# Windowed attention and channel mixing: low parts of weights and the first unit's mixing on TensorE and ScalarE

## The chip, the cores and the metric

The kernel runs on one core of one Trainium2 chip. The metric is device time in microseconds (us) of one execution. The engines have short names here, as in the profile: PE is TensorE (PEld its weight loads), DVE is VectorE, ACT is ScalarE, POOL is GpSimd, SP is SyncE. SBUF is the on-chip memory, PSUM the banks in which PE leaves its results.

## The reference

Causal attention over a window of 64 positions, for 8 batches, 8 heads, 576 positions and head size 64, followed by a channel mixing layer with 512 model and 1024 inner columns, all in float32:

```
scores = scale * q @ k.T        # only where 0 <= i - j < 64
attn   = softmax(scores)
x      = attn @ v               # heads side by side: (8, 576, 512)
x_prev = x one position earlier, 0 at the start of a batch
xk = mu_k * x + (1 - mu_k) * x_prev
xr = mu_r * x + (1 - mu_r) * x_prev
k  = relu(xk @ w_k)
out = sigmoid(xr @ w_r) * ((k * k) @ w_v)
```

The weights come in as 64-bit floating point numbers, which the chip's engines do not compute with.

## The kernel before, in words

**Split operands.** Each weight and each activation of the three big products is held as two numbers of the kind fp32r: a high part (the value rounded by a copy to fp32r) and a low part (the value less its high part). A product is three fp32r matmuls instead of one: high by high, high by low, low by high (`product`, lines 578 to 594). fp32r matmuls are PE's fast form for four-byte numbers here; plain fp32 matmuls are used for the scores, the transposes and the values.

**Weights.** There are 28 chunks of 128 rows (`chunks`, line 198): 0 to 3 of w_r and 4 to 11 of w_k with 512 columns, 12 to 27 of w_v with 256. Each is loaded once as pairs of 32-bit words (`load_w`) and decoded on the chip (`decode`, lines 220 to 259): ACT takes the absolute value of the upper word (`sign`); DVE clamps, shifts, and joins the bits of both words in four steps (`clamp`, `shift`, `upper`, `lower`), so that the tile `wt` holds the weight as fp32; ACT copies it to fp32r (`first_part`, tile `w`); DVE subtracts that from `wt` (`second_part`) and has the low part. All products of unit 0 wait for the chunks they use.

**Attention.** 72 blocks of 64 positions are handled in 36 groups of two. A group is a burst of 32 score matmuls on PE (`scores`, PSUM tile `s`), a softmax on DVE and ACT (`soften`), four transposes on PE (`flip`, tile `t`), two masked copies on DVE (`keep`, tile `pt`), and 64 value matmuls on PE (`values`, tile `x`), which ACT copies into `xu`. For the groups in `LEAN` the softmax saves two wide DVE steps (`less` and `total`): ACT does eight exponentials of 64 columns with a bias and a sum each (`exps`) in place of one wide exponential.

**Mixing and products.** The positions are also cut into 11 units of 4, 5 and then nine times 7 blocks (256, 320 and 448 columns). For each unit, `mix` (lines 510 to 568) makes xk and xr for each of four chunks of 128 model columns. In units 0 and 1 ACT scales the shifted x by 1 - mu (`before`, tile `e`), DVE adds mu times x (`blend`), ACT makes the high part and DVE the low part. `r_units`, `k_units` and `v_units` follow with 48, 96 and 96 matmuls each and ACT and DVE steps behind them.

**What sets the order.** The kernel describes every step as a `Piece`: an engine, a key, an estimated cost, what it needs, and which buffers it takes and uses. `play` (lines 106 to 161) runs through them once when the program is built: whenever an engine is free in its estimate, it begins the piece with the lowest key whose needs and buffers are there. The order that results is the order of the instructions on each engine; on the chip each engine takes its own instructions strictly in that order and waits where data are late. Keys come from `BEGIN` (one per group), `DECODE` (one per chunk) and the numbers in the main loop. Buffers that count here: six tiles `tmp` for decoding and mixing, three PSUM banks `m` for the products, two tiles each for queries and keys, three for values.

**Queues.** Every load and store is issued by SP's queue: first the early loads in the order of lines 685 to 701, with the keys -9999 and up, then the later groups' loads (`prefetch`) and the stores. A value load is four transfers of 64 KB, eight where the two blocks lie in different batches. GpSimd makes the constants (the identity `ident`, masks) at the start and zeroes the first column of some units' `xu`; else it is idle.

All pieces are recorded by a helper at line 75, so the profile shows that line for nearly all instructions, and tiles tell them apart.

Of the kernel before, what the change touches and what calls it, by code (L numbers as in the profile page):

```python
# [41 lines left out]
BEGIN = (-30, -28, -8, 4, 12, 30, 40, *range(53, 184, 10),  # L42
         196, 210, 223, 236, 250, 263, 277, 286, 295, 304, 312, 322, 332, 342, 352)
# [11 lines left out]
def attn_rwkv_kernel(ctx, tc, qT, kT, v2, mu_k, mu_r, w_k, w_v, w_r, out):  # L55
# [50 lines left out]
    def play():  # L106
# [11 lines left out]
        while any(left.values()):  # L118
# [10 lines left out]
            for e, ps in left.items():  # L129
                if free[e] > now:  # L130
                    continue
                for i, (_, n, p) in enumerate(ps):
# [18 lines left out]
                    if p.size:  # L151
                        bus = max(p.done + 1300, bus) + p.size / RATE
                        p.lag = bus + 500 - p.done
# [36 lines left out]

    muk = const.tile([P, NC], F32, name="muk")
# [28 lines left out]
    def decode(n, loaded):  # L220
# [27 lines left out]
        def second_part():  # L248
            LOW[1].tensor_sub(ws[i, c][:, 1], words[n], ws[i, c][:, 0].bitcast(F32))

        LOW = ("POOL", pool) if n in POOL_LOW else ("DVE", dve)
# [6 lines left out]
        decoded[id(ws), i, c] = p0, Piece(LOW[0], key, (30 + 2.43 * wc) if LOW[0] == "POOL" else 70 + 1.05 * wc,  # L258
                                          second_part, [p0], uses=[word], port=True)
# [4 lines left out]
    def transfer(fn, size, takes=(), needs=(), key=None, count=1):  # L264
        return Piece("SP", len(pieces) - 9999 if key is None else key, 450 * count, fn, needs, takes, size=size)

    def load(what, g, key=None):
# [13 lines left out]
        def fn():  # L281
            x = loaded[what, g] = ld.tile(shape, F32, name=what, bufs=bufs)
            if what == "q" and b0 == b1:
                dma.dma_start(x, columns(qT, b0, i0, 2))
            elif what == "q":
                dma.dma_start(x[:, :, :W], columns(qT, b0, i0, 1))
                dma.dma_start(x[:, :, W:], columns(qT, b1, i1, 1))
            elif what == "k":
                o = int(i0 == 0)
                if b0 == b1:  # L290
                    dma.dma_start(x[:, :, o * W:], columns(kT, b0, i0 - 1 + o, 3 - o))
                else:
                    dma.dma_start(x[:, :, :2 * W], columns(kT, b0, i0 - 1, 2))
                    dma.dma_start(x[:, :, 2 * W:], columns(kT, b1, i1, 1))
            else:
                for p in range(2):
                    for j in range(2):
                        if b0 == b1:
                            dma.dma_start(x[p * W:(p + 1) * W, j], value(b0, i0, p, 2)[:, j])
                        else:  # L300
                            dma.dma_start(x[p * W:(p + 1) * W, j, 0], value(b0, i0, p, 1)[:, j, 0])
                            dma.dma_start(x[p * W:(p + 1) * W, j, 1], value(b1, i1, p, 1)[:, j, 0])

        count = {"q": 1, "k": 1, "v": 2}[what] * (1 + (b0 != b1))
        if what == "v":
            count *= 2
        arrived[what, g] = transfer(fn, 6 * P * {"q": 8, "k": 12, "v": 8}[what] * W, [held[what, g]], key=key,
                                    count=count)
# [107 lines left out]
    def soften(key, g, p, bank):  # L416
# [65 lines left out]
        if lean:  # L482
            q = Piece("ACT", key + 0.5, 8 * 225, exps, [q], uses=[bank])
# [6 lines left out]
        q = Piece("PE", key + 1, 430, flip, [q], [tbank], [rows], lag=200, kind="t", slack=slow(key))  # L490
# [19 lines left out]
    def mix(u, c, key, xk, xr):  # L510

        n = UNITS[u] * W
        d, todo = [], [(xk, muk, muk1, Hold("tmp")), (xr, mur, mur1, Hold("tmp"))]
        pk = None
        LOW = ("POOL", pool) if u in POOL_MIX else ("DVE", dve)
# [14 lines left out]
        for (xs, hold, made), mu, mu1, own_ in todo:  # L530
# [24 lines left out]
            def low(e=e, xs=xs):  # L555
                LOW[1].tensor_sub(xs[0][:, 1, c, :n], e[0][:, :n], xs[0][:, 0, c, :n].bitcast(F32))

            if u >= 2:
                p = Piece("DVE", key, over(n) + 70, blend, [pk], [own_], [held["x", u], scratch], port=True)
            else:  # L560
                p = Piece("ACT", key, acts(n) + 60, before,
# [3 lines left out]
                p = Piece("DVE", key, over(n), blend, [p], uses=[held["x", u]], port=True)  # L565
# [200 lines left out]
```

## Time and profile before

| what | value |
|---|---|
| median of 3 runs | 659.18 us (658.49 to 660.22) |
| profiled execution | 660.74 us |
| its span, first to last instruction | 659.0 us |
| mean granted clock of PE | 0.987 |
| PE busy | 614.9 us, 93% of the span, 6112 matmuls |
| DVE busy | 445.1 us, 68%, 945 instructions |
| ACT busy | 350.8 us, 53%, 765 instructions |
| POOL busy | 3.5 us, 1%, 25 instructions |
| DMA | 53.39 MB, mean 81 GB/s over the span |

In the profile's rows, `m<-xk,w 128*128 128x256` is a matmul that writes tile `m` from `xk` and `w` with a 128 by 128 array and 256 columns; `x12` counts instructions; the first two numbers of a row in order of time are its start and its duration in us; what stands in brackets is the idle time ahead of it and what ended that. The duration of a DVE or ACT row overlaps the next one's start by some 0.1 us. A row of a grouped view ends with the idle time before its instructions and what ended most of it. Shares of busy time are averages over the span, and the start differs much from the rest.

### The profile page before, as it was taken

To read this page: it belongs to the slowest core of one execution; us is meant where nothing else is said; L and a number is where in the kernel's file an instruction comes from. 1 tells how busy PE (TensorE), PEld (TensorE's weight loads), DVE (VectorE), ACT (ScalarE), POOL (GpSimd) and SP (SyncE) were. 2 spreads that over 40 slices of the span, in tenths; PEclk is the share of its full clock that TensorE was granted. 3 is DMA by queue.
4 is the path that set the end of the run, shared out by engine and by line. 5 is a ranking of instruction groups with operands and counts; after the bars stand their busy time and mean duration, and the time that the engine had idled before them with its cause. 6 is when DMAs were issued, how large, how long until landed. Compare 5 with 4: busy or idle time off the path is not lost.

```text
span 659.0 us, 14734 instructions
## 1 busy us (share of the span) xinstructions
PE 614.9 (93%) x6112; PEld 562.6 (85%) x6112; DVE 445.1 (68%) x945; ACT 350.8 (53%) x765; POOL 3.5 (1%) x25
## 2 busy tenths in 40 slices
PE   2566679999999999999999999999999999999997
PEld 2456678999999999999999999999999999999997
DVE  4998898697569559757944945884697578245221
ACT  3768675744753563475266436536734652661750
POOL 1000000000000000000000000000000000000000
PEclk9998889999999999999999999999999999999999
DMA  8992211323224222332311321231233201001001
GB/s 237 288 350 77 58 57 38 100 78 97 59 62 128 71 58 81 99 95 57 99 34 50 92 66 50 71 114 41 64 96 118 63 18 57 1 1 42 15 1 56
DMA packets 77410, 53.39 MB, mean 81 GB/s; under 512 B 12832, under 2 KB 73760, under 8 KB 77344
## 3 DMA queue, kind: packets, MB, share of 16 engines
q1 hardware_dynamic: 77344, 52.45, 26.6%
q8 instruction: 48, 0.79, 0.5%
q14 instruction: 18, 0.15, 0.1%
HBM read 43.00 MB, written 9.44 MB: 80 GB/s over the span
## 4 chain that ended last, share of the span: by engine, by line
PE 87%; DVE 6%; DMA 3%; ACT 2%; issue 1%; SPq 0%; ACTq 0%
PE m L75 74%; PE s L75 5%; PE x L75 5%; PE t L75 3%; DMA w<-w_r 2%; DVE wt L75 2%; DMA w<-w_k 1%; DVE w L75 1%; ACT pr L75 1%; DVE e L75 1%; ACT w L75 0%; DVE most L75 0%; DVE xr L75 0%; DVE s L75 0%; DVE r L75 0%
## 5 line engine op out<-in xcount | busy, mean ns | idle before, releaser
L75 PE MATMUL m<-xk,w 128*128 128x448 f32 (+2 forms) x1056 | 219.8, 359 | 7.1 <-ACT kf L75 6.3
L75 PE MATMUL m<-ks,w 128*128 128x448 f32 (+2 forms) x1056 | 215.1, 356 | 4.0 <-DVE ks L75 2.2
L75 PEld LDWEIGHTS m<-xk,w 128*128 128x128 f32 x1056 | 189.4, 192 | 21.5 <-ACT kf L75 6.9
L75 PEld LDWEIGHTS m<-ks,w 128*128 128x128 f32 x1056 | 188.0, 190 | 17.8 <-DVE ks L75 2.4
L75 DVE TENSOR_TENSOR ks<-kf,ks 128x448 fp32r<-128x448 f32 (+2 forms) x88 | 52.2, 594 | 103.8 <-ACT ks L75 103.6
L75 PE MATMUL m<-xr,w 128*128 128x448 f32 (+2 forms) x528 | 116.2, 366 | 3.6 <-ACT xr L75 1.8
L75 PEld LDWEIGHTS m<-xr,w 128*128 128x128 f32 x528 | 97.1, 197 | 13.0 <-ACT xr L75 2.9
L75 ACT ACTIVATE kf<-m 128x448 f32<-128x448 f32 (+2 forms) x88 | 45.8, 520 | 91.5 <-PE m L75 90.0
L75 ACT CAST xk<-e 128x448 fp32r<-128x448 f32 (+2 forms) x44 | 23.8, 541 | 71.7 <-DVE e L75 71.6
L75 DVE TENSOR_TENSOR pt<-t,sides 128x512 f32<-128x512 f32 x72 | 48.1, 685 | 12.4 <-PE t L75 12.4
L75 PE MATMUL s<-k,q 64*64 64x128 f32 (+1 forms) x1152 | 42.3, 289 | 12.9 <-ACT pr L75 7.2
L75 DVE SCALAR_TENSOR_TENSOR r<-th,r 128x448 f32<-128x448 f32 (+2 forms) x44 | 26.1, 593 | 40.5 <-ACT r L75 40.4
L75 PEld LDWEIGHTS s<-k,q 64*64 64x64 f32 x1152 | 33.3, 145 | 22.7 <-issue 10.3
L75 ACT ACTIVATE kf<-kf 128x448 f32<-128x448 f32 (+2 forms) x88 | 48.8, 555 | 2.6
L75 ACT CAST ks<-kf 128x448 fp32r<-128x448 f32 (+2 forms) x88 | 47.8, 543 | 2.7
L75 PE MATMUL x<-pt,v 64*64 64x64 f32 x2176 | 41.0, 227 | 3.7 <-ACT w L75 2.1
L75 PEld LDWEIGHTS x<-pt,v 64*64 64x64 f32 x2176 | 39.3, 143 | 5.0 <-ACT w L75 2.4
L75 ACT COPY xu<-x 128x512 f32<-128x512 f32 (+1 forms) x44 | 22.1, 513 | 36.5 <-PE x L75 36.2
L75 DVE SCALAR_TENSOR_TENSOR r<-m,r 128x448 f32<-128x448 f32 (+2 forms) x44 | 25.8, 587 | 22.0 <-PE m L75 21.8
L75 ACT ACTIVATE th<-m 128x448 f32<-128x448 f32 (+2 forms) x44 | 22.9, 520 | 29.2 <-PE m L75 28.8
L75 PE MATMUL t<-ident,pr 128*128 128x128 f32 x144 | 24.0, 293 | 9.1 <-DVE pr L75 9.1
L75 ACT CAST xr<-e 128x448 fp32r<-128x448 f32 (+2 forms) x44 | 23.9, 543 | 15.3 <-DVE e L75 14.9
(47 smaller groups left out, 509.5 us busy)
## 6 DMA issues: line engine op xcount, KB each, us to landing
k<-kT SPq DMA_DIRECT2D x28, 384.0 KB, 3.8
q<-qT SPq DMA_DIRECT2D x32, 256.0 KB, 3.1
v<-v SPq DMA_DIRECT2D x128, 64.0 KB, 2.6
w<-w_k SPq DMA_DIRECT2D x8, 512.0 KB, 6.9
w<-w_v SPq DMA_DIRECT2D x16, 256.0 KB, 5.6
outT<-r SPq DMA_DIRECT2D x12, 224.0 KB, 1.9
k<-kT SPq DMA_DIRECT2D x8, 256.0 KB, 3.2
w<-w_r SPq DMA_DIRECT2D x4, 512.0 KB, 5.7
```

The source lines that it names most:

```text
L75: return lambda *args, **kw: tc.keep_in_program_order(op(*args, **kw))
```

## The change

Five things change, all of them in the start of the program.

1. **Low parts of 13 chunks** (`PE_LOW`: 0 to 11 and 19). PE multiplies the decoded fp32 weight by the identity, adds the product of the negative identity `minus` and the high part in the same PSUM bank `m`, and ACT copies the bank to the low part. For the other chunks DVE subtracts as before.
2. **Mixing of unit 0** (`PE_MIX`). Instead of ACT's scaling and DVE's blend, PE multiplies x and the shifted x by diagonal matrices with mu and 1 - mu (`mixer`, 16 of them, made by ACT from the identity) into one bank `m`, in plain fp32. ACT takes the high part from there, DVE the low part.
3. **Queues.** The values of groups 0 to 5 are issued by GpSimd, mu_k and mu_r by ACT; GpSimd makes 1 - mu in place of DVE.
4. **Order of the early loads** (`ORDER`): weights come forward one by one, the keys of group 4 come last.
5. **Keys and estimates**: `BEGIN`, `DECODE`, the mixing's keys and some estimated costs are new numbers; the lean softmax is used for groups 1, 2, 3, 4, 5 and 8 in place of 0 to 4.

```diff
+BEGIN = (-31, -27, -10, 4, 12, 22, 41, 51, 63, 71, 87, 93, 103, 113, 123, 133, 143, 153, 163, 173, 183, 196,
+    210, 223, 236, 250, 263, 277, 286, 295, 304, 312, 322, 332, 342, 352)
+DECODE = (-31, -28, -23, -22, -18, -11, -7, -7, -5, -1, 0, 3, 7, 8, 9, 10, 11, 12, 12, 14, 15, 16, 17, 21, 19,
+    20, 21, 25)
+MIX_0 = (-32, -1, 2, 2)
+MIX_1 = (29, 32, 40, 55)
+PE_LOW = {0, 1, 2, 3, 4, 5, 6, 7, 8, 9, 10, 11, 19}
+PE_MIX = {0}
+LEAN = {1, 2, 3, 4, 5, 8}
+LOADED = 6
+ORDER = (*"w q0 k0 w V0 q1 k1 w w w w w q2 V1 w w k2 V2 w w w q3 w w k3 V3 w w w w w w q4 w w w w w w".split(),
+         *"V4 w w q5 k5 V5 k4".split())
...
+        def rest_of():
+            ps.append(ps_m.tile([P, 512], F32, name="m", tag="m")[:, :wc])
+            pe.matmul(ps[0], ident, words[n], start=True, stop=False)
+            pe.matmul(ps[0], minus, ws[i, c][:, 0], start=False, stop=True)
+
+        def take_rest():
+            sca.copy(ws[i, c][:, 1], ps[0])
...
+        if n in PE_LOW:
+            p = Piece("PE", key, 5 * (1.5 + .453 * wc), rest_of, [p0, made_minus], [bank], [word], lag=200, kind="m")
+            p = Piece("ACT", key, acts(wc), take_rest, [p], (), [bank])
+        else:
+            p = Piece("DVE", key, 70 + 1.05 * wc, second_part, [p0], uses=[word], port=True)
...
+        return Piece(engine, len(pieces) - 9999 if key is None else key, {"SP": 500, "POOL": 1000}[engine] * count, fn,
+                     needs, takes, size=size)
...
+                def blended(ps=ps, w=w):
+                    ps.append(ps_m.tile([P, 512], F32, name="m", tag="m")[:, :n])
+                    (_, _, _, x0), = parts(u)
+                    pe.matmul(ps[0], mixer[:, w, 0, c], xs_of[u][:, c, x0:x0 + n], start=True, stop=False)
+                    pe.matmul(ps[0], mixer[:, w, 1, c], xs_of[u][:, c, x0 - 1:x0 - 1 + n], start=False, stop=True)
+
+                def high(ps=ps, xs=xs, hold=hold):
+                    if not xs:
+                        xs.append(act.tile([P, 2, NC, TU], F32R, name=hold.tag))
+                    sca.copy(xs[0][:, 0, c, :n], ps[0])
+
+                def low(ps=ps, xs=xs):
+                    dve.tensor_sub(xs[0][:, 1, c, :n], ps[0], xs[0][:, 0, c, :n].bitcast(F32))
...
     def vectors():
-        dma.dma_start(muk, mu_k)
-        dma.dma_start(mur, mu_r)
-
-    def rest():
-        dve.tensor_scalar(muk1, muk, -1.0, 1.0, op0=ALU.mult, op1=ALU.add)
-        dve.tensor_scalar(mur1, mur, -1.0, 1.0, op0=ALU.mult, op1=ALU.add)
...
+        sca.dma_start(muk, mu_k)
+        sca.dma_start(mur, mu_r)
+
+    def opposite():
+        pool.tensor_scalar(muk1, muk, -1.0, 1.0, op0=ALU.mult, op1=ALU.add)
+        pool.tensor_scalar(mur1, mur, -1.0, 1.0, op0=ALU.mult, op1=ALU.add)
+
+    def mixers(c):
+        for w, mus in enumerate(((muk, muk1), (mur, mur1))):
+            for a, mu in enumerate(mus):
+                sca.mul(mixer[:, w, a, c], ident, mu[:, c:c + 1])
+
+    made_minus = Piece("ACT", -99, 200, lambda: sca.mul(minus, ident, -1.0))
+    p = Piece("ACT", -98, 200, vectors, lag=2500)
+    arrived["mu"] = Piece("POOL", -98, 250, opposite, [p], port=True)
+    made_mixer = [Piece("ACT", MIX_0[c] - 1, 800, lambda c=c: mixers(c), [arrived["mu"]]) for c in range(NC)]
+    for what in ORDER:
+        if what == "w":
+            load_w(1)
+        else:
+            load(what[0].lower(), int(what[1]), engine="POOL" if what[0] == "V" else "SP")
```

More of the change, by code (lines that the diff above doesn't have):

```diff
@@ L306, in load @@
             count *= 2
-        arrived[what, g] = transfer(fn, 6 * P * {"q": 8, "k": 12, "v": 8}[what] * W, [held[what, g]], key=key,
-                                    count=count)
+        arrived[what, g] = transfer(fn, 5 * P * {"q": 8, "k": 12, "v": 8}[what] * W, [held[what, g]], key=key,
+                                    count=count, engine=engine)
     def block(g, s):
@@ L482, in soften @@
         if lean:
-            q = Piece("ACT", key + 0.5, 8 * 225, exps, [q], uses=[bank])
+            q = Piece("ACT", key + 0.5, 8 * 290, exps, [q], uses=[bank])
         else:
@@ L489, in soften @@
         q = Piece("DVE", key + 0.5, 610, scale, [q], uses=[sm], port=True)
-        q = Piece("PE", key + 1, 430, flip, [q], [tbank], [rows], lag=200, kind="t", slack=slow(key))
+        q = Piece("PE", key + 1, 430, flip, [q], [tbank], [rows], lag=300, kind="t", slack=slow(key))
         q = Piece("DVE", key + 1, 610, lambda: keep(1), [q], [kept], [tbank])
@@ L512, in mix @@
         n = UNITS[u] * W
+        if u in PE_MIX:
+            for w, (xs, hold, made) in enumerate((xk, xr)):
+                ps, bank = [], Hold("m")
+                def blended(ps=ps, w=w):
[9 more added lines that the diff above has]
+                    dve.tensor_sub(xs[0][:, 1, c, :n], ps[0], xs[0][:, 0, c, :n].bitcast(F32))
+                p = Piece("PE", key, 8 * (1.5 + .453 * n), blended,
+                          {got[t] for t in range(FIRST[u], FIRST[u + 1])} | {made_mixer[c], mixing.get((u, w))},
+                          [bank], [held["x", u]], lag=200, kind="m")
+                mixing[u, w] = p
+                p = Piece("ACT", key, acts(n), high, [p], [hold] if c == 0 else [])
+                made.append((p, Piece("DVE", key, over(n), low, [p], (), [bank])))
+            return
         d, todo = [], [(xk, muk, muk1, Hold("tmp")), (xr, mur, mur1, Hold("tmp"))]
         pk = None
-        LOW = ("POOL", pool) if u in POOL_MIX else ("DVE", dve)
         if u >= 2:
@@ L555, in low @@
             def low(e=e, xs=xs):
-                LOW[1].tensor_sub(xs[0][:, 1, c, :n], e[0][:, :n], xs[0][:, 0, c, :n].bitcast(F32))
+                dve.tensor_sub(xs[0][:, 1, c, :n], e[0][:, :n], xs[0][:, 0, c, :n].bitcast(F32))
             if u >= 2:
-                p = Piece("DVE", key, over(n) + 70, blend, [pk], [own_], [held["x", u], scratch], port=True)
+                p = Piece("DVE", key, over(n) + 130, blend, [pk], [own_], [held["x", u], scratch], port=True)
             else:
-                p = Piece("ACT", key, acts(n) + 60, before,
+                p = Piece("ACT", key, acts(n) + 115, before,
                           {got[t] for t in range(FIRST[u], FIRST[u + 1])} | {arrived["mu"], mixing.get(u)},
@@ L564, in mix @@
                 mixing[u] = p
-                p = Piece("DVE", key, over(n), blend, [p], uses=[held["x", u]], port=True)
+                p = Piece("DVE", key, over(n) + 60, blend, [p], uses=[held["x", u]], port=True)
             p = Piece("ACT", key, acts(n) + 20, high, [p])
-            made.append((p, Piece(LOW[0], key, over(n) if LOW[0] == "DVE" else 40 + 2.45 * n, low, [p], uses=[own_],
-                                  port=True)))
+            made.append((p, Piece("DVE", key, over(n), low, [p], uses=[own_], port=True)))
     mixing = {}
@@ L718, in attn_rwkv_kernel @@
         if u == 0:
[L719 removed]
+            keys = MIX_0
         elif u == 1:
[L721 removed]
+            keys = MIX_1
         else:
```

66 lines of the change are left out of this document (19 added, 47 removed).

## The prediction, made before the result was known

> **What bounds the kernel now.** I read three views in this order. First the table of busy time by stretches, cut at 28.4 us (where the mixing of unit 0 begins) and at 107 us:
>
> ```profile
> 0.00:28.40 28.40, 9.51 (x186) 7.53 (x186) 18.59 (x43) 14.46 (x47) 2.76 (x18) 1.00 0.88 265
> 28.40:107.00 78.60, 57.05 (x566) 50.93 (x566) 72.49 (x194) 54.75 (x171) 0.21 (x2) 0.89 0.41 131
> 107.00:655.50 548.50, 548.38 (x5363) 504.15 (x5363) 353.50 (x709) 281.56 (x549) 0.53 (x5) 1.00 0.22 64
> ```
>
> Columns: stretch, length, busy us of PE, PEld, DVE, ACT, POOL, granted clock, DMA share, GB/s. From 107 us on PE is busy 548.38 of 548.50 us: whatever the change does, this stretch needs the same PE work, so the end moves with its start. Between 28.4 and 107 us DVE is busy 72.49 of 78.60 us (92%), PE 57.05: DVE paces this stretch and PE idles 21.55 us in it. ACT (54.75) has room. Before 28.4 us PE idles 18.9 us, and no PE work can replace it cheaply, since little has arrived.
>
> Second, the chain of waits, which agrees for both early stretches:
>
> ```profile
> 2.38 7.93 DMA w<-w_r
> 11.19 4.66 DMA w<-w_r
> 15.87 8.06 DMA w<-w_k
> 23.96 0.69 DVE wt L75
> ...
> 106.96 2.46 PE m L75 x15
> ...
> 560.55 94.85 PE m L75 x468
> ```
>
> Weight transfers carry the first 24 us, then mostly DVE steps of decoding, softmax and mixing; from 106.96 us the chain is PE to the end. So the question is by how much the start of that row moves.
>
> Third, the instructions of PE in order of time, for its real speed in the start:
>
> ```profile
> 47.25 1.99 PE L75 MATMUL s<-k,q 64*64 64x128 f32 x32
> 63.44 2.93 PE L75 MATMUL m<-xk,w 128*128 128x256 f32 x12 [4.57 <-ACT kf L75]
> 69.54 0.90 PE L75 MATMUL s<-k,q 64*64 64x128 f32 x32
> 74.79 1.64 PE L75 MATMUL m<-xk,w 128*128 128x256 f32 x12 [0.78 <-ACT kf L75]
> 80.50 1.08 PE L75 MATMUL t<-ident,pr 128*128 128x128 f32 x4 [4.07 <-DVE pr L75]
> 109.32 0.63 PE L75 MATMUL t<-ident,pr 128*128 128x128 f32 x4
> ```
>
> The same work takes about 1.8 times as long after a pause (2.93 against 1.64 us, 1.99 against 0.90): a PE that waits is also a slow PE, and its busy time in the start holds some of that.
>
> **What DVE gets rid of.**
>
> ```profile
> 14.89 0.69 DVE L75 TENSOR_TENSOR w<-wt,w 128x512 fp32r<-128x512 f32 x1
> 15.49 0.68 DVE L75 SCALAR_TENSOR_TENSOR wt<-w,wt 128x512 uint32<-128x512 uint32 x1
> 30.18 0.48 DVE L75 SCALAR_TENSOR_TENSOR e<-xu,mur,e 128x256 f32<-128x256 f32 x1
> 30.57 0.42 DVE L75 TENSOR_TENSOR xk<-e,xk 128x256 fp32r<-128x256 f32 x1
> 30.91 0.69 DVE L75 SCALAR_TENSOR_TENSOR wt<-w,wt 128x512 uint32<-128x512 uint32 x1
> ```
>
> Durations overlap the next instruction, so I count from start to start: a 512-wide low part 0.60 us (14.89 to 15.49), a 256-wide one 0.34 (30.57 to 30.91), a blend of unit 0 0.39 (30.18 to 30.57). The change takes 12 x 0.60 + 0.34 + 8 x 0.39 = 10.7 us off DVE. Three wide low parts lie before 28.4 us (1.8 us); 8.9 us lie behind. With DVE at 92%, 8.9 us of work is 8.9 x 78.60 / 72.49 = **9.7 us** of that stretch, if nothing else paces it. The lean softmax moves from group 0 to group 5: group 0 gains two wide DVE steps (1.2 us, less 0.1 for a tiny one), group 5 loses them; zero over the start. Group 8's saving falls where PE paces: nothing. The DVE low parts of unit 0 stay. The new keys move the bursts of groups 0 to 10 by at most eight key steps (group 5, 30 to 22); they issue the same instructions, so I count them at nothing: what they shift inside the start is covered by whatever else is ready, and without that cover it lies within the bounds below.
>
> **What PE gets.** A low part is one plain fp32 matmul of 512 columns with the identity and one fp32r matmul; a mix is two fp32 matmuls of 256 columns. No row shows a plain full-array fp32 matmul. The nearest is the transpose, four fp32 matmuls against the identity, 512 columns together: 0.63 us at speed, 1.08 after a pause. The fp32r one, as 2 of 12 in the rows above per 256 columns: 0.27 and 0.49. So a 512-wide low part costs 0.90 to 1.57 us, a mix 0.63 to 1.08. In the second stretch, 9 low parts, half a one, and 8 mixes: 9.5 x (0.90 to 1.57) + 8 x (0.63 to 1.08) = **13.6 to 23.6 us**. I take 20, nearer the slow end, since the six transposes of the start took 6.1 us together, 1.02 each:
>
> ```profile
> L75 PE MATMUL t<-ident,pr 128*128 128x128 f32 x24 | 6.1, 401 | 9.1 <-DVE pr L75 9.1
> ```
>
> Of the 21.55 us idle that leaves 1.5. A PE that waits less runs faster, though:
>
> ```profile
> L75 PE MATMUL m<-xk,w 128*128 128x256 f32 x96 | 16.5, 336 | 6.7 <-ACT kf L75 6.3 <-ACT r L75 0.3
> L75 PE MATMUL m<-ks,w 128*128 128x256 f32 x96 | 14.0, 307 | 4.0 <-DVE ks L75 2.2 <-ACT kf L75 1.5 <-DVE r L75 0.3
> L75 PE MATMUL m<-xr,w 128*128 128x256 f32 x48 | 12.5, 415 | 3.6 <-ACT xr L75 1.8 <-DVE xr L75 1.4 <-ACT r L75 0.3
> ```
>
> These 240 matmuls are busy 43.0 us; at 1.64/12 each they would take 32.8. I take half of the 10.2 back, 5. So PE lets the stretch shrink by 1.5 + 5 = **6.5 us** (bounds: none at 23.6 us without any faster clock; more than DVE's 9.7 at 13.6 us).
>
> The Trainium skill (FP8 and Floating Point Precision, section TensorE Precision Notes) speaks against the change here: true FP32 takes four passes through the array. The transpose row, 0.63 us against 0.27, shows little more than two; if a plain matmul follows the page, the first rival's sum holds.
>
> **What ACT gets.** Thirteen copies out of PSUM and 16 small scalings for the mixers come, eight scalings of unit 0 go:
>
> ```profile
> L75 ACT COPY xu<-x 128x512 f32<-128x512 f32 x4 | 2.4, 600 | 3.4 <-PE x L75 3.4
> L75 ACT ACTIVATE e<-xu,mu 128x256 f32<-128x256 f32 x8 | 4.1, 508 | 2.1 <-DVE w L75 1.2 <-DVE xk L75 0.5 <-DVE xr L75 0.4
> L75 ACT ACTIVATE pr<-s,most 128x64 f32<-128x64 f32 x40 | 11.9, 325 | 2.9 <-DVE most L75 2.8
> ```
>
> 12.5 x 0.60 + 16 x 0.33 + the negative identity 0.33 - 4.1 = +9.0 us, between 64-wide and 256-wide rows for the scalings (0.33 to 0.51, +12 at most). Under the 37 us in which ACT is idle before 107 us this costs nothing as work. As a chain it does: a low part now goes ACT, PE, ACT. Each such handing over is covered by other chunks in flight.
>
> **The queues.** On SP 28 value transfers and two tiny ones go:
>
> ```profile
> 0.80 0.44 SPq L75 DMA_DIRECT2D q<-qT  x1
> 2.85 3.11 SPq L75 DMA_DIRECT2D v<-v  x4
> 10.71 0.91 SPq L75 DMA_DIRECT2D w<-w_r  x2
> ```
>
> The third and fourth weight chunk were issued at 10.71 us, behind values, keys and mu; now they can go several us sooner. But DVE, not yet short of chunks once it has two, has only 1.8 us less to do there, and the first scores come later behind a weight chunk: I count **zero** for the first stretch, bounds -2 and +2. GpSimd takes the values up, in this order on its queue: constants, values 0, 1, 2 (three buffers are free at once), then the two tiny subtractions for mu, which the mixers of chunk 0 on ACT need. The planner lets these mixers go ahead of everything on ACT.
>
> ```profile
> 3.53 0.10 POOL L75 MEMSET xu<- 128x4 f32 x1
> 10.33 0.67 ACT L75 ACTIVATE wt<-w 128x512 f32<-128x512 f32 x1 [1.12 <-DMA w<-w_r]
> 10.90 0.30 ACT L75 ACTIVATE pr<-s,most 128x64 f32<-128x64 f32 x1
> ...
> 8.42 0.17 DVE L75 TENSOR_SCALAR most<-most 128x8 f32<-128x8 f32 x1
> ...
> v<-v SPq DMA_DIRECT2D x128, 64.0 KB, 2.6
> ```
>
> POOL is free at 3.6 us. Twelve issues at SP's 3.11/4 = 0.78 us end at 13.0 us; at the 2.6 us from the issue of a value transfer to its landing (last row), at 35 us. The issue is nearer the first; I take 1.0, the planner's figure, so 15.6 us. The plan has them over after 12 us; counted from SP's first issue at 0.80 us ACT would stand some 2.8 us before the mixers. Behind it stand the exponentials of group 1 and the next chunks' first step; the rows show such a wait at work (the exponentials, ready at 8.6 us, began at 10.90 behind a weight). DVE has chunks at hand for about half of that: **1.5 us** lost (0 to 20). Values 3 to 5 wait on GpSimd for a free buffer; behind them stands only the zeroing of a later unit's first column, which has slack.
>
> The Trainium skill (SBUF — State Buffer, section SBUF: two separate sides) warns that DVE operations on two ports keep GpSimd from writing its descriptors, so that a transfer of 620 ns took about 3100 ns in its example; at that the twelve issues would end near 41 us. No run here shows it yet.
>
> **The sum.** The stretch shrinks by the smaller of DVE's 9.7 and PE's 6.5, less 1.5 for ACT's wait: 5.0 us. The profiled execution took 660.74 us (span 659.0 and 1.74 around it): 655.7. It stands 1.56 above the median of 659.18, so on that scale **654.2 us**.
>
> **The rivals.** *PE takes DVE's place and loses more than it gains.* Place: PE between 28.4 and 107 us. If a plain fp32 matmul costs four times the fp32r one (1.09 to 1.95 us for 512 columns), the added work is 9.5 x (1.36 to 2.44) + 8 x (1.09 to 1.95) = 21.6 to 38.8 us. Halfway, 30.2, against 21.55 + 5 of room, is 3.7 us too much, and with ACT's 1.5 the time is 659.18 + 5.2 = 664.4 us. It decides from 26.5 us of added work. For it: the many slow rows, and three PSUM banks now shared by products, low parts and mixes. Against: such a full PE would run at speed, where 21.6 fits.
>
> *No change.* The twelve issues of GpSimd take 1.5 us each, the mu subtractions end at 21.6 us, ACT stands 8.8 us before the mixers; DVE's chunks at hand cover some 2.3, and the other 6.5 eat what PE allows: 659.2 us. For it: ACT's strict order in the rows. Against: the landing row is a transfer, not an issue.
>
> *DVE alone decides.* The added matmuls cost their lower bound, 13.6 us, PE has room for all, no wait at the mixers: -9.7 and some of the first stretch's 1.8, say -10.5: 648.7 us. Against: PE and DVE feed each other through six buffers, and both would have to be busy above 90%.
>
> **How the numbers follow.** Forecast 0.46 (its own range 650.5 to 657), PE as bound 0.22, no change 0.18, DVE alone 0.14. A measurement of this kernel tells about 0.3% (2 us) from no change. Faster 0.60, same 0.18, slower 0.22. From 647.5 to 661.5 us the range holds the forecast, no change, most of DVE alone and the mild part of the slower rival; some 2 in 10 lie outside.
>
> **What would show it.** Right: PE's unbroken chain begins 4 to 6 us earlier than 106.96; DVE below 90% and PE above 80% between 28 and 102 us; the 512-column fp32 matmul near 1 us; products of 256 columns below 43 us busy. Wrong: that matmul near 2 us or the chain of the start on PE low parts and mixes (first rival); ACT idle several us before its scalings of the mixers, released by POOL (no change); PE waiting for values. If the unbroken stretch itself gets longer, the whole argument fails.

## The result and the profile after

The changed kernel takes **642.41 us** (median), the kernel before 658.84 us on the same chip: a ratio of **0.9748** (95% interval 0.9733 to 0.9763). On the scale of 659.18 us that is 16.6 us less (15.6 to 17.6). The profiled execution took 642.39 us, its span is 640.6 us.

The table of busy time by stretches, after (columns as before):

```profile
0.00:28.40 28.40, 15.73 (x194) 9.46 (x195) 19.55 (x43) 18.00 (x50) 11.02 (x34) 0.76 0.94 319
28.40:107.00 78.60, 75.69 (x917) 66.05 (x918) 74.64 (x203) 66.58 (x216) 8.61 (x17) 1.00 0.44 131
107.00:637.00 530.00, 529.97 (x5075) 486.42 (x5073) 337.44 (x677) 272.75 (x539) 0.53 (x5) 1.00 0.22 64
```

Between 28.4 and 107 us PE idles 2.9 us instead of 21.55. The same stretch now holds 917 matmul records where it held 566. PE pays for that with little busy time: over the whole span 621.4 us after 614.9. DVE is still 95% busy there.

The chain of waits, after:

```profile
2.26 7.36 DMA w<-w_r
9.64 12.95 DMA w<-w_k
22.60 10.04 DMA w<-w_v
32.64 0.40 DVE xr L85
33.04 2.15 DVE wt L85 x5
...
82.68 3.00 PE m L85 x24
85.69 0.52 PE t L85 x4
86.21 2.61 PE m L85 x21
...
542.12 94.86 PE m L85 x468
```

Three weight transfers, then DVE's steps from 32.6 us on, then PE to the end. PE's part now begins at 82.7 us. A sharper mark is the first product of unit 1 (128x320 columns). It starts at 105.11 us in the trace of before and at 86.74 us after. DVE's last low part of a weight and the rows of PE behind it, before:

```profile
100.63 0.42 DVE L75 TENSOR_TENSOR w<-wt,w 128x256 fp32r<-128x256 f32 x1
...
101.85 3.09 PE L75 MATMUL m<-ks,w 128*128 128x256 f32 x24 [0.29 <-DVE r L75]
105.11 1.58 PE L75 MATMUL m<-xk,w 128*128 128x320 f32 x9 [0.17 <-DVE r L75]
```

and after:

```profile
85.34 0.42 DVE L85 TENSOR_TENSOR w<-wt,w 128x256 fp32r<-128x256 f32 x1
...
85.58 0.63 PE L85 MATMUL t<-ident,pr 128*128 128x128 f32 x4
85.96 0.94 PE L85 MATMUL m<-ks,w 128*128 128x256 f32 x6
86.74 0.59 PE L85 MATMUL m<-xk,w 128*128 128x320 f32 x3
```

That is 18.4 us earlier, and the span is 18.4 us shorter (659.0 to 640.6): behind the mark both kernels take 553.9 us, with nearly the same work on PE (after, nine products of unit 0 more and four transposes less). (The profiled execution of before stands 1.56 us above its median, so the medians differ by less, and up to that much of the terms below belongs to this one execution.) All of the gain lies ahead of the mark, and DVE's account tells where. I cut it at 20 us and at the end of DVE's last low part, which is at 101.05 us before and at 85.76 us after. Stretches of before, and what DVE waited for in the second one (us in total, times, longest):

```profile
0.00:20.00 20.00, 6.43 (x116) 4.95 (x116) 11.49 (x28) 9.07 (x35) 2.76 (x18) 1.00 0.81 234
20.00:101.05 81.05, 54.91 (x598) 48.97 (x599) 73.63 (x197) 57.63 (x179) 0.11 (x1) 0.89 0.50 159
```

```profile
DVE w L75 <- ACT w L75: 3.0, 4, 1.2
DVE pt L75 <- PE t L75: 2.6, 4, 1.7
DVE rs L75 <- ACT pr L75: 1.5, 4, 0.6
```

The same two views of after:

```profile
0.00:20.00 20.00, 8.76 (x78) 4.50 (x78) 11.59 (x26) 9.69 (x25) 10.24 (x32) 0.86 0.90 283
20.00:85.76 65.76, 61.42 (x724) 50.26 (x725) 64.50 (x181) 60.80 (x208) 9.28 (x17) 0.94 0.57 185
```

```profile
DVE xk L85 <- ACT xk L85: 0.4, 1, 0.4
DVE rs L85 <- ACT pr L85: 0.4, 1, 0.4
```

The 18.4 us are three terms:

- DVE's work from 20 us on: 73.63 to 64.50, **9.1 us**.
- DVE's waits there: 81.05 - 73.63 = 7.4 us to 1.3, **6.2 us**. The largest, `w <- ACT w` (3.0 us), is one that a low part on DVE brings with it: it has to wait for ACT's high part, and everything behind it in DVE's order stands with it. The wait for the transposes (2.6 us) went too. But the new order alone ends most of the waits as well: in e1 below, with all low parts still on DVE, 2.8 us are left.
- From the last low part to the mark: 101.05 to 105.11 is 4.06 us, 85.76 to 86.74 is 0.98, **3.1 us**. This is no idle time: DVE is busy all through it in both kernels and PE nearly so. Before, 24 products of unit 0 (3.09 us of PE) stand there in PE's order; after, 6.

The first 20 us gave nothing: DVE works 11.5 and 11.6 us in them.

### The profile page after: what moved, and what is told of

Same layout as the page of the kernel before. It is cut to its first block, busy times and chain, and to the rows that moved or that the text cites. A ratio compares the mean times of both kernels' runs of the same rounds, so it can differ in the third digit from the quotient of the medians.

```text
span 640.6 us, 14909 instructions
## 1 busy us (share of the span) xinstructions
PE 621.4 (97%) x6183; PEld 561.9 (88%) x6183; DVE 432.3 (67%) x921; ACT 357.3 (56%) x802; POOL 20.2 (3%) x55
## 4 chain that ended last, share of the span: by engine, by line
PE 87%; DVE 5%; DMA 5%; ACT 2%; issue 1%; SPq 0%; ACTq 0%
PE m L85 75%; PE s L85 5%; PE x L85 4%; DVE wt L85 3%; PE t L85 2%; DMA w<-w_k 2%; DMA w<-w_v 2%; DMA w<-w_r 1%; ACT kf L85 1%; DVE w L85 0%; ACT pr L85 0%; DVE pt L85 0%; DVE most L85 0%; DVE r L85 0%; ACT w L85 0%
## 5 line engine op out<-in xcount | busy, mean ns | idle before, releaser
L85 PE MATMUL m<-xk,w 128*128 128x448 f32 (+2 forms) x1056 | 215.8, 354 | 0.2 <-ACT kf L85 0.2
L85 PE MATMUL m<-ks,w 128*128 128x448 f32 (+2 forms) x1056 | 212.5, 353 | 0.1
L85 PEld LDWEIGHTS m<-xk,w 128*128 128x128 f32 x1056 | 185.9, 188 | 13.6 <-ACT kf L85 0.5
L85 PE MATMUL m<-xr,w 128*128 128x448 f32 (+2 forms) x528 | 111.8, 355 | 0.9 <-ACT r L85 0.7
L85 PEld LDWEIGHTS m<-xr,w 128*128 128x128 f32 x528 | 93.9, 188 | 8.6 <-ACT r L85 1.0
L85 ACT CAST xk<-e 128x448 fp32r<-128x448 f32 (+1 forms) x40 | 22.4, 560 | 69.4 <-DVE e L85 69.0
L85 PEld LDWEIGHTS s<-k,q 64*64 64x64 f32 x1152 | 30.4, 135 | 20.3 <-issue 19.9
L85 PE MATMUL s<-k,q 64*64 64x128 f32 (+1 forms) x1152 | 38.8, 273 | 9.4 <-DMA k<-kT 9.4
L85 ACT CAST xr<-e 128x448 fp32r<-128x448 f32 (+1 forms) x40 | 22.4, 561 | 15.3 <-DVE e L85 15.1
L85 DVE COPY_PREDICATED s<-own,s 128x512 f32<-128x512 uint32 (+1 forms) x44 | 24.0, 545 | 8.6 <-PE s L85 8.2
```

The source lines that it names most:

```text
L85: return lambda *args, **kw: tc.keep_in_program_order(op(*args, **kw))
```

## The experiments

Each run lists its ratio to the kernel before on the same chip; differences in us are that ratio times 659.18. Diffs are against the changed kernel unless said otherwise. For all of them I made the same account of DVE as above; it is collected here, worked out from the stretches and rows in order of time of each trace. "Gap" is the time from DVE's last low part to the mark, "rest" that from the mark to the end of the span. (One kernel, e10, makes no low part of a weight on DVE and stands in the text alone.)

| kernel | ratio (95%) | DVE work 0-20 | work from 20 | idle from 20 | gap | mark | rest |
|---|---|---|---|---|---|---|---|
| before | 1 | 11.5 | 73.6 | 7.4 | 4.1 | 105.1 | 553.9 |
| after | 0.9748 (0.9733-0.9763) | 11.6 | 64.5 | 1.3 | 1.0 | 86.7 | 553.9 |
| old engines (e1) | 0.9940 (0.9921-0.9958) | 10.9 | 75.9 | 2.8 | 1.1 | 99.8 | 554.9 |
| mixing only (e3) | 0.9904 (0.9880-0.9928) | 11.2 | 72.1 | 4.2 | 1.0 | 97.4 | 554.9 |
| low parts only (e2) | 0.9842 (0.9824-0.9861) | 12.3 | 67.4 | 5.1 | 1.0 | 93.5 | 554.5 |
| old plan (e4) | 0.9838 (0.9823-0.9852) | 8.5 | 65.8 | 2.1 | 3.6 | 91.5 | 555.3 |
| old keys (e4b) | 0.9845 (0.9822-0.9868) | 11.9 | 61.8 | 6.8 | 6.3 | 94.9 | 554.6 |
| old loads (e5b) | 0.9837 (0.9817-0.9858) | 7.9 | 67.8 | 4.6 | 1.6 | 94.0 | 553.8 |
| values on SP (e5) | 0.9798 (0.9778-0.9817) | 10.6 | 65.8 | 1.9 | 1.0 | 88.7 | 553.8 |
| DVE doubled (e6) | 0.9841 (0.9827-0.9856) | 13.0 | 71.5 | 0.8 | 1.0 | 93.3 | 553.8 |
| PE doubled (e7) | 0.9836 (0.9820-0.9853) | 11.0 | 65.4 | 6.9 | 1.0 | 93.3 | 553.8 |
| plain fp32 (e11) | 0.9815 (0.9795-0.9834) | 11.4 | 65.1 | 5.4 | 1.0 | 91.5 | 553.8 |
| no PE low parts (e14) | 0.9790 (0.9768-0.9811) | 12.0 | 64.4 | 4.4 | 1.0 | 89.7 | 553.9 |
| before, ACT low parts (e13) | 0.9866 (0.9849-0.9884) | 11.3 | 66.8 | 4.2 | 4.1 | 95.1 | 553.9 |
| other estimates (e9) | 0.9821 (0.9804-0.9838) | 11.4 | 65.9 | 5.7 | 1.0 | 92.6 | 553.7 |
| one back on DVE (e15) | 0.9836 (0.9820-0.9852) | 11.2 | 65.3 | 1.4 | 3.2 | 89.9 | 553.9 |
| two back on DVE (e16) | 0.9828 (0.9811-0.9846) | 10.7 | 66.9 | 1.9 | 3.2 | 92.0 | 553.8 |

**Which half of the change.** The old division of work with the new keys, loads and queues (e1):

```diff
-PE_LOW = {0, 1, 2, 3, 4, 5, 6, 7, 8, 9, 10, 11, 19}
-PE_MIX = {0}
+PE_LOW = set()
+PE_MIX = set()
```

> The changed kernel with its new keys, load order and queues, but DVE makes all low parts and ACT and DVE mix unit 0, as before. Theory 'order': of the 16.4 us gained, some 10 are DVE work taken away and some 6 come from the new order, so this run stands near 652 us. Theory 'clock': the 6 us come from a PE that the added matmuls keep busy and so at full speed; without them the time is near 658 us, and the 240 matmuls of 256 columns are busy some 43 us again instead of 33. If the order gives most of it: under 648 us.

It took 655.75 us, 4.0 us less than before: between the two expectations. DVE's waits from 20 us on fall from 7.4 us to 2.8 and the gap from 4.1 to 1.1, though DVE does no less; the 240 products of 256 columns are busy 39.6 us (43.0 before, 33.0 after). The new division of work with the old keys, old order of loads and the values on SP (e4; mu stays on ACT's queue, and the planner's estimates stay the new ones, as in e1):

```diff
-BEGIN = (-31, -27, -10, 4, 12, 22, 41, ...
+BEGIN = (-30, -28, -8, 4, 12, 30, 40, ...
...
-LEAN = {1, 2, 3, 4, 5, 8}
+LEAN = {0, 1, 2, 3, 4}
...
-            load(what[0].lower(), int(what[1]), engine="POOL" if what[0] == "V" else "SP")
+            load(what[0].lower(), int(what[1]), engine="SP")
```

> The changed kernel's work on PE and ACT, but the old keys, the old choice of lean groups, the old order of the early loads, and the values issued by SP. Theory 'order': only DVE's 10 us are gained, near 648 to 649 us. Theory 'clock': nearly all is kept, 642 to 645 us, with the 256-column matmuls near 33 us busy.

648.83 us, 10.7 us less, as theory 'order' had it. So the engines' work alone is worth 10.7 us, the plan alone 4.0, and both together 16.6, 1.9 more than the sum, which is no more than the intervals (about 1 us each) leave open. In e4 the 240 products are as fast as after the change (32.1 us busy), and it is still 5.9 us slower than the changed kernel: PE's speed alone does not make that difference. Each half of the new division alone, with the new plan, e2 (the first pair of lines) and e3 (the second):

```diff
-PE_MIX = {0}
+PE_MIX = set()
...
-PE_LOW = {0, 1, 2, 3, 4, 5, 6, 7, 8, 9, 10, 11, 19}
+PE_LOW = set()
```

> The changed kernel, but unit 0 is mixed by ACT and DVE as before; PE still makes the 13 low parts. DVE gets 8 x 0.39 = 3.1 us back and PE loses 8 x 0.86 = 6.9 us. Since both doublings (of a DVE step, of a PE step) cost nearly their full work: if DVE counts 1:1, 645.5 us; if the relief of PE pays for it, 642 us or less.

> The changed kernel, but DVE makes all low parts; PE still mixes unit 0. DVE gets 7.5 us back, PE loses 12 x 1.10 + 0.5 = 13.7 us. If DVE counts 1:1: 650 us. If a PE with fewer matmuls also falls back to half speed: up to 654. If the relief of PE pays for half: 646.

Low parts alone took 649.53 us, mixing alone 653.41, each more than DVE's work one to one (645.5 and 650): 6.5 us and 2.4 us less than e1, 8.9 together, where both in one give 12.7. (The interval of mixing alone overlaps that of e1, so its 2.4 us are not clear of noise.) In e2 and e3 DVE idles 4 to 5 us from 20 us on, in the changed kernel 1.3. The plan's keys suit the whole and lose part of it with either half.

**Keys, loads, queue.** With the new division of work, e4b puts back only the old keys and lean groups, e5b only the old order of loads and SP for the values, e5 only SP for the values (e4b's lines, then those of e5b, of which e5 has the last pair):

```diff
-BEGIN = (-31, -27, -10, 4, 12, 22, 41, ...
+BEGIN = (-30, -28, -8, 4, 12, 30, 40, ...
...
-LEAN = {1, 2, 3, 4, 5, 8}
+LEAN = {0, 1, 2, 3, 4}
...
-ORDER = (*"w q0 k0 w V0 q1 k1 w w w w w q2 V1 ...
+ORDER = "q0 k0 w w V0 q1 k1 w w V1 w w w w q2 k2 V2 ...
...
-            load(what[0].lower(), int(what[1]), engine="POOL" if what[0] == "V" else "SP")
+            load(what[0].lower(), int(what[1]), engine="SP")
```

> The changed kernel with the old keys and the old choice of lean groups; load order and queues stay new. The old plan as a whole (keys, loads, queue) cost 6.4 us. If the keys are behind it: 648 us. If loads and queue are: 642 to 643.5.

> The changed kernel with the old order of the early loads and the values issued by SP; keys stay new. If loads and queue are behind the 6.4 us: 648 us. If the keys are: 642 to 643.5.

> The changed kernel with one thing put back: the values of all units are issued by SyncE's queue again, in the new order of loads and with the new keys. Theory A (keys and order of loads belong together, and the queue is only a means): the values' issues, 0.6 to 0.8 us each on SP, come between the weight loads, which moves the first chunks by 1 to 3 us; the time is 643 to 645 us, and the last low part on DVE ends at 86 to 88 us. Theory B (it is the queue that keeps the weight loads early): the time is 648 to 650 us, as with the old order of loads, and PE and DVE are again idle before 20 us.

649.34, 649.30 and 645.27 us, the last close to theory A. New keys without new loads, or new loads without new keys, are no better than neither (e4). With old loads DVE works 7.9 us in the first 20 instead of 11.6; with old keys it is early enough but waits 6.8 us later and the gap before the mark is 6.3. Only the pair gains. The queue, at the new order, is worth 3.3 us.

**What a microsecond costs, in one and the same order.** In the next four kernels every engine keeps the changed kernel's order of instructions, since the planner's estimates are left alone; only durations differ. e6 does `upper` twice for the 13 chunks (7.5 us more on DVE):

```diff
             dve.scalar_tensor_tensor(word, raw[n][:, :, 1], 0xC0000000, word, op0=ALU.bitwise_and, op1=ALU.bitwise_or)
+            if n in PE_LOW:
+                dve.scalar_tensor_tensor(word, raw[n][:, :, 1], 0xC0000000, word, op0=ALU.bitwise_and,
+                                         op1=ALU.bitwise_or)
```

> The changed kernel in which DVE does the third decoding step (upper) twice for the 13 chunks whose low part PE makes: 12 x 0.60 + 0.34 = 7.5 us more on DVE, same order, same result. If DVE still paces the start: 642.4 + 7.5 = 650 us. If PE paces it since the change: under 644 us. Halfway (both): 646.

649.02 us, 6.1 us more than the changed kernel by the ratios: four fifths of DVE's added work. e7 does the identity's matmul twice:

```diff
+            pe.matmul(ps[0], ident, words[n], start=True, stop=True)
             pe.matmul(ps[0], ident, words[n], start=True, stop=False)
             pe.matmul(ps[0], minus, ws[i, c][:, 0], start=False, stop=True)
```

> The changed kernel in which PE multiplies the decoded weight by the identity twice for the 13 chunks (the first result is overwritten): 12 x 0.46 + 0.24 = 5.8 us more on PE at full speed, twice that at half speed, same order, same result. If PE paces the start: 642.4 + 5.8 = 648 us. If DVE paces it: under 644 us.

648.74 us, 5.8 us more. That this is just the 5.8 us of the expectation is luck: at the price found below, 0.86 us for a plain matmul of 512 columns, the added work is 10.8 us. DVE's work did not grow (65.4 us from 20 us on, 64.5 in the changed kernel), its idle time did, from 1.3 to 6.9. The same DVE steps in order of time, of the changed kernel:

```profile
31.68 0.42 DVE L85 TENSOR_TENSOR xk<-m,xk 128x256 fp32r<-128x256 f32 x1 [0.41 <-ACT xk L85]
...
35.16 0.69 DVE L85 COPY_PREDICATED s<-own,s 128x512 f32<-128x512 uint32 x1
...
48.70 0.42 DVE L85 TENSOR_TENSOR xr<-m,xr 128x256 fp32r<-128x256 f32 x1
```

and of e7:

```profile
33.41 0.42 DVE L85 TENSOR_TENSOR xk<-m,xk 128x256 fp32r<-128x256 f32 x1 [1.53 <-ACT xk L85]
...
38.60 0.69 DVE L85 COPY_PREDICATED s<-own,s 128x512 f32<-128x512 uint32 x1 [1.63 <-PE s L85]
...
54.97 0.42 DVE L85 TENSOR_TENSOR xr<-m,xr 128x256 fp32r<-128x256 f32 x1 [1.89 <-ACT xr L85]
```

DVE falls 1.7, 3.4 and 6.3 us behind, each time at a step that takes a result of PE (mixing and scores), and stays 6.5 behind from then on. So PE's added work is not paid by the microsecond; it is paid where a DVE step waits for it.

e11 reads the second matmul of a low part as plain fp32 too:

```diff
-            pe.matmul(ps[0], minus, ws[i, c][:, 0], start=False, stop=True)
+            pe.matmul(ps[0], minus.bitcast(F32), ws[i, c][:, 0].bitcast(F32), start=False, stop=True)
```

> The changed kernel with the second matmul of a low part (negative identity times the high part) read as plain fp32, like the first, in place of fp32r. In the trace of the changed kernel the plain one takes 0.46 us for 512 columns in two records, the fp32r one 0.64 in one. Theory A (the 0.64 is a weight load that stands uncovered where the two types change): the low part falls from 1.10 to 0.92 us, 13 x 0.18 = 2.3 us of PE work go, at 0.55 us of time for a us 1.3 us: 641 us. Theory B (the 0.64 is the price of a matmul that follows another one into the same bank, whatever its type): the low part stays at 1.1 us or grows, 642 to 643 us.

646.81 us: 4.4 us more, the side of theory B and beyond it. It settles the price of a plain matmul. PE in order of time, changed kernel:

```profile
31.70 1.02 PE L85 MATMUL m<-wt,ident 128*128 128x512 f32 x2
32.16 0.80 PE L85 MATMUL m<-w,minus 128*128 128x512 f32 x1
32.80 1.02 PE L85 MATMUL m<-wt,ident 128*128 128x512 f32 x2
```

and e11:

```profile
32.84 1.02 PE L85 MATMUL m<-wt,ident 128*128 128x512 f32 x2
33.70 1.02 PE L85 MATMUL m<-w,minus 128*128 128x512 f32 x2
34.55 1.02 PE L85 MATMUL m<-wt,ident 128*128 128x512 f32 x2
```

From start to start a plain fp32 matmul of 512 columns takes 0.86 us. A whole low part takes 1.10 us (31.70 to 32.80), so the fp32r one takes 0.24. My reading in the expectation, 0.46 for the plain and 0.64 for the fp32r one, took the start stamp of the second matmul for the end of the first; it was wrong, and with it the idea of an uncovered weight load.

e14 takes the 26 matmuls out, and ACT copies the high part in place of the result, so the low parts aren't computed:

```diff
         def rest_of():
-            ps.append(ps_m.tile([P, 512], F32, name="m", tag="m")[:, :wc])
-            pe.matmul(ps[0], ident, words[n], start=True, stop=False)
-            pe.matmul(ps[0], minus, ws[i, c][:, 0], start=False, stop=True)
+            pass

         def take_rest():
-            sca.copy(ws[i, c][:, 1], ps[0])
+            sca.copy(ws[i, c][:, 1], ws[i, c][:, 0].bitcast(F32))
```

> The changed kernel without the 26 matmuls of the 13 low parts, in the same order of everything else; ScalarE copies the high part in their place (what the rounding left is left out of the computation). PE loses 13 x 1.10 = 14 us of work, DVE and ACT do as before. Theory A (both engines pace the start, PE at 0.55 us of time for a us, as when the identity's matmul was doubled): -7.9, 634 to 635 us. Theory B (after the change DVE alone paces, PE's part is hidden): 640 us or more. Theory C (PE alone paces): 628 to 629 us.

645.59 us: with 14 us of PE work gone, the kernel is 2.8 us **slower** than the changed one. No theory foresaw a loss: theory B's "640 us or more" covers the time, but PE work that is merely hidden would have left 642.4. PE in order of time, e14:

```profile
29.66 3.78 PE L85 MATMUL m<-xu,mixer 128*128 128x256 f32 x8 [1.32 <-ACT xu L85]
33.37 1.81 PE L85 MATMUL s<-k,q 64*64 64x128 f32 x32
...
44.53 3.95 PE L85 MATMUL m<-xu,mixer 128*128 128x256 f32 x8
```

and the changed kernel:

```profile
28.81 0.79 PE L85 MATMUL m<-w,minus 128*128 128x512 f32 x1
29.87 1.99 PE L85 MATMUL m<-xu,mixer 128*128 128x256 f32 x8 [0.27 <-ACT xu L85]
...
33.98 1.10 PE L85 MATMUL s<-k,q 64*64 64x128 f32 x32
```

Eight records of the mixing take 1.99 us behind low parts and 3.78 behind a pause. What DVE waits for from 20 us on, e14:

```profile
DVE rs L85 <- ACT pr L85: 0.9, 1, 0.9
DVE xk L85 <- ACT xk L85: 0.9, 1, 0.9
DVE xr L85 <- ACT xr L85: 0.7, 1, 0.7
```

With the low parts gone PE is at about half speed in several rows, mixes and scores come later, and DVE idles 3.1 us more (4.4 against 1.3). The order on DVE is the same in both, so its delay can be followed step by step: 0.5 us at the first `xk`, 1.3 at the first `xr` behind it, 1.7 at transposes near 42 us. The rest, up to 3.0 us, comes after 59 us at steps that wait for ACT, which itself stood 1.4 us for products of PE (`th <- PE m`). ACT's 12 wide copies also take 0.03 us more each than those out of PSUM, 0.4 us in all, and that was not separated.

The slowness itself is shown by the durations; its cause is not. The granted clock in the profile is 0.65 to 0.67 from 40 to 50 us, where eight records of the mixing take 3.95, but 1.00 from 30 to 35, where most of the 3.78 lie. The Trainium skill (TensorE: Matmul & The Clock Gate, section Part 1: The HAM clock gate) says that after an idle window of about 3.4 us the array gets half its clock. The factors here, 3.78 to 1.99 and 1.81 to 1.10, are near a half, but from 20 us to the second slow row PE never pauses for more than 2.4 us at a time.

**DVE's relief without PE's work.** e13 starts from the kernel **before**: the 12 wide low parts leave DVE, ACT copies the high part instead (the subtraction is left out of the computation), PE gets nothing:

```diff
         def second_part():
+            if wc == 512:
+                sca.copy(ws[i, c][:, 1], ws[i, c][:, 0].bitcast(F32))
+                return
             LOW[1].tensor_sub(ws[i, c][:, 1], words[n], ws[i, c][:, 0].bitcast(F32))
```

> The kernel before with the 12 low parts of 512 columns taken off DVE and given to ScalarE alone: a copy of the high part in place of the difference (what the chunk's rounding left is left out of the computation). DVE -7.2 us, ACT +7.2 us, PE nothing; old keys, loads and queues. Theory A (what DVE gets rid of comes off the time one to one, PE's new work is free): 7 us, 652 us, and the price for a us of DVE is the same as where PE took the work over. Theory B (PE's work in the changed kernel costs 0.55 us a us, so that without it the gain is larger): 9 us or more for the same DVE work, 650 us or less, and the slow products of 256 columns get faster by themselves.

650.76 us, 8.8 us less for 7.2 us of DVE work. The account says why it is more than one to one: 6.8 us of work and 3.2 us of waits go (7.4 to 4.2; the wait `w <- ACT w` falls from 3.0 to 0.9). Together that is the 10.0 us by which the two traces differ; the medians differ by 1.2 less, since the profiled execution of before took 1.56 us more than its median. The planner's order moved in part with the change (98 of DVE's 933 other instructions stand at another place), so not all of the 3.2 us need be the step's own. The time lies nearer theory B, but for another reason than B gave. The 240 products of 256 columns fall from 43.0 to 38.4 us busy with no PE work added (13.8, 13.9 and 10.7): so part of PE's speed comes back when DVE delivers sooner. The opposite control, added PE work without use in the kernel before (e12), has no measurement, so what a faster PE alone would give there stays open.

**Other orders and other shares.** e9 gives the planner smaller estimates for the new matmuls, e10 gives all 28 low parts to PE, e15 and e16 take chunk 0, and chunks 0 and 1, off PE (in this order):

```diff
-            p = Piece("PE", key, 5 * (1.5 + .453 * wc), rest_of, ...
+            p = Piece("PE", key, 3 * (1.5 + .453 * wc), rest_of, ...
...
-                p = Piece("PE", key, 8 * (1.5 + .453 * n), blended,
+                p = Piece("PE", key, 4 * (1.5 + .453 * n), blended,
...
-PE_LOW = {0, 1, 2, 3, 4, 5, 6, 7, 8, 9, 10, 11, 19}
+PE_LOW = set(range(28))
...
+PE_LOW = {1, 2, 3, 4, 5, 6, 7, 8, 9, 10, 11, 19}
...
+PE_LOW = {2, 3, 4, 5, 6, 7, 8, 9, 10, 11, 19}
```

> The changed kernel with the planner told smaller costs for the new matmuls (3 in place of 5 for a low part, 4 in place of 8 for a mix; 0.7 and 0.47 us, against measured 1.10 and 0.86); the engines do the same work, only the written-out order moves. Theory A (the order is robust, the gain comes from where the work is done): 641.5 to 643.5 us. Theory B (the new keys are fitted to that one order, as old keys or old loads alone cost 6 to 7 us): 645 to 649 us, with DVE's and PE's idle before the last low part on DVE larger by 3 us or more.

> The changed kernel with the low parts of all 28 weight chunks on TensorE and ScalarE, 15 more than before. Off DVE go 15 x 0.60 = 9 us, onto PE come 15 x 1.10 = 16.5 us. Theory A (both engines pace the start, DVE at 0.85 us of time for a us of work, PE at 0.55, as doubling their work gave): -7.7 + 9.1, so some 644 us. Theory B (DVE alone paces the start): 634 to 636 us. Theory C (PE is full from 28 us on, with 2.9 us idle): all but that is paid, 654 to 656 us.

> The changed kernel with the low part of chunk 0 back on DVE. Theory A (after 20 us DVE is full and sets the end; before 20 us it is idle 8.4 us, waiting for transfers and for scores behind a PE at half speed, so that 0.6 us of DVE work cost nothing there and a PE with 2 us less to do at half speed hands its scores over sooner): 641 to 642.5 us, with the same 64 to 65 us of DVE work from 20 us to its last low part. Theory B (the written-out order and its fit count for more than where one low part is made): 645 to 649 us, as in the other runs whose order moved, with DVE idle 4 to 6 us after 20 us in place of 1.3.

> The same with chunks 0 and 1 back on DVE. Theory A: 641 to 643 us (the second low part lies at 14 to 18 us, where DVE still waits 1.0 us for a weight's first step). Theory B: 645 to 649 us.

646.81, 653.24, 648.03 and 647.58 us. e9 does the same work in another order and loses 4.8 us: theory B there, DVE idle 5.7 us. e10 loses 11.3 us, close to theory C; its expectation counted the 15 further chunks as wide, but all are 256 columns, so DVE lost half as much work as stated there, and it idles 8.4 us of the 77.1 between 20.0 us and 97.1, just ahead of its mark at 98.1. In e15 and e16 DVE is as full as theory A said (idle 1.4 and 1.9 us), but 3.2 us lie between the last low part and the mark, so theory B's time came out with theory A's DVE; in e15 the profiled execution took 645.48 us and the other three 647.9 to 648.3, so the trace shows some 2.5 us less than a typical run. What fills the gap can be read from both traces: 24 products of unit 0 stand in PE's order between the last low part and the mark, as in the kernel before, where the changed kernel has 6, and PE and DVE are both busy. Why the planner's order comes out so there wasn't traced. No version beat the changed kernel.

## Why the prediction was wrong

The forecast was 654.2 us (range 647.5 to 661.5); it came out at 642.4, on the right side and beyond the range. The step that failed is the ceiling of 9.7 us on what DVE can give, together with the keys counted at nothing: the traces show 18.4 us, of which only 9.1 are DVE's work, 6.2 its waits and 3.1 products of PE that stood in the gap. The term for PE's speed was mis-sized too (5 us taken, 10.0 measured), but that alone would not have saved the sum: with it, and without the wait of ACT that did not occur, the smaller of the two limits is still 9.7 us, so 649.5 us.

- **What bounds the kernel now**: right. From the mark on PE needs the same 553.9 us, and 553.6 to 555.3 in every experiment. DVE paced the start, and still does: e6 pays for four fifths of what it adds to DVE, and e14 gains nothing from less work on PE. The sign named for it, DVE below 90% busy, did not come (95%).
- **What DVE gets rid of**: the work was right (10.7 us counted; 9.1 from 20 us on, and 12.8 over the span, 445.1 to 432.3, with group 8 and the mu step). The step that made 9.7 us of it, as the most that DVE can give, failed: it scaled DVE's idle by the same share as its work. DVE's idle was waits in a strict order, 7.4 us of it behind 20 us, of which 6.2 went; with the division of work alone (e4) 2.1 were left, with the new plan alone (e1) 2.8. The quoted share of 92% busy hid that.
- **What PE gets**: the size was near, the way to it was not. For the 9.5 low parts and 8 mixes that the forecast of 20 us counts, the measured prices give 9.5 x 1.10 + 8 x 0.86 = 17.3 us at full speed, inside its bounds (a mix at 0.86 is two plain matmuls of 256 columns; all low parts and mixes of the start come to 12 x 1.10 + 0.55 + 8 x 0.86 = 20.6). The transposes were no measure of a plain matmul: four of them have 512 columns together, and the start of the next product lies only 0.38 us behind theirs (85.58 to 85.96). As that product is of another kind, I count over the neighbours instead: from the last product start ahead of them (85.41) to the second behind (86.16) 0.75 us pass, of which two products take 0.115 each, so 0.52 for the transposes, and 0.44 by the same count in the full stretch (138.9 us). A plain matmul takes 0.86. That is 3.6 times the fp32r one's 0.24, close to the four passes that the Trainium skill states (FP8 and Floating Point Precision, section TensorE Precision Notes). The "little more than two" that the prediction read from the transposes was no price of a plain matmul; the page came nearer. What saved the sum: I had the fp32r matmul too dear (0.27 to 0.49) and took a high value.
- **"I take half of the 10.2 back, 5"**: the mis-sized term. After, in lines by form up to 100 us:

```profile
L85 PE MATMUL m<-xk,w 128*128 128x256 f32 x96 | 12.8, 282 | 0.2 <-ACT kf L85 0.2
L85 PE MATMUL m<-ks,w 128*128 128x256 f32 x96 | 12.2, 280 | 0.1
L85 PE MATMUL m<-xr,w 128*128 128x256 f32 x48 | 8.0, 296 | 0.9 <-ACT r L85 0.7
```

  33.0 us instead of 43.0: PE got back 10.0 of the 10.2. With that, PE's own sum (1.5 us idle and 10) would have allowed 11.5 us, not 6.5.
- **The smaller of DVE and PE**: the step behind both. PE was set against DVE as a rival for the end of the stretch. In fact PE acts on DVE through waits: more PE work (e7, e11) and less PE work (e14) both lose, and the sign depends on whether a mix or a score comes late. Taking the minimum of two sums left out that the two feed each other, and that DVE waits longer for a slower PE (e14).
- **The first stretch at zero, the keys at nothing**: right for the first as a net (11.5 and 11.6 us of DVE work in 20 us; with the old loads, e4 and e5b, it is 8.5 and 7.9, so the new loads fill the place of the low parts), wrong for the second. The plan alone is worth 4.0 us (e1), and 3.1 us of the gain is the gap before the mark, which no step of mine had. With the old plan it is 3.6 to 4.1 us, with the new one mostly 1.0.
- **ACT's wait before the mixers, 1.5 us**: did not occur. POOL's issues, after:

```profile
3.36 2.47 POOL L85 DMA_DIRECT2D v<-v  x4
...
5.91 2.32 POOL L85 DMA_DIRECT2D v<-v  x4
10.32 0.76 POOL L85 DMA_DIRECT2D v<-v  x1 [2.10 <-DMA v<-v]
12.12 1.74 POOL L85 DMA_DIRECT2D v<-v  x3 [1.04 <-DMA v<-v]
13.94 0.18 POOL L85 TENSOR_SCALAR mu<-muk 128x4 f32<-128x4 f32 x1
```

  An issue takes 0.6 us, not 1.0, and SP's take as long: the 0.78 was the mean of a row of four, one of which took 1.07. The mu step is done at 14.3 us, ahead of ACT, which stands for the next weight until 15.06:

```profile
15.06 0.67 ACT L85 ACTIVATE wt<-w 128x512 f32<-128x512 f32 x1 [2.84 <-DMA w<-w_r]
15.63 0.39 ACT L85 ACTIVATE mixer<-ident,muk 128x128 f32<-128x128 f32 x1
```

  The starvation of GpSimd's descriptors of which the Trainium skill warns (SBUF — State Buffer, section SBUF: two separate sides) does not show: the first eight issues take 0.58 to 0.72 us each, and the four behind them, with DVE busy, 0.58 to 0.76. These twelve land 5.9 to 7.8 us after their issue, the same transfers from SP in e5 4.0 to 8.7. Whether DVE's steps there are of the kind that the page means, the trace doesn't show. The move to that queue gains 3.3 us (e5).
- **The rivals**: PE as the bound and no change fell. "DVE alone decides" was nearest in mechanism and 6.3 us short in size (648.7), since it too had DVE's work and not its waits.

What is left open: why old keys with new loads, or the reverse, lose the whole 6 us was seen in DVE's idle and gap, not traced to one step. What PE's speed alone, at unchanged waits, is worth was not separated; e14 shows only what less work on PE costs here, and e4 that full speed alone does not bring the whole gain.

## What to carry to other kernels

On an engine that works in a strict order, count what it waits for beside what it does: a step taken off it can take its wait along. In the old plan, with no work added to PE (e13), 3.2 us of waits went with 6.8 us of work; with a new order besides, 6.2 with 9.1. Work given to an idle PE can cost less than nothing, as here, where taking it away slowed PE's other matmuls, as long as no result of PE that others wait for becomes late; test it in both directions at a fixed order. An order fitted to one division of work loses several us when anything moves, so try a division and its order together, and read a matmul's price from one start to the next of its own kind.

## What the runs showed of the hardware that was not expected

- A plain fp32 matmul of 512 columns takes 0.86 us at speed and shows as two records and two weight loads; an fp32r one takes 0.24. The start of the next matmul of another kind lies only 0.46 us behind the plain one's, so the split between the two can't be read from their start stamps.
- Four fp32 transposes of 128 columns take 0.44 to 0.52 us between full neighbours, a little over half of a plain matmul with as many columns. The Trainium skill (TensorE: Matmul & The Clock Gate, section Terms) calls the transpose mode four times faster for FP32; here it is 0.86 to 0.44 or 0.52, a factor of 1.7 to 2.0.
- Taking 14 us of matmuls out of the start, in which PE is not quite full, made the kernel 2.8 us slower (e14), and adding some 20 us to the whole raised PE's busy time by 6.5.
- GpSimd issues a 64 KB value transfer in 0.6 us, as SP does (0.60 for most of the early ones in e5), with DVE at work beside it.
